# Inverse root mean squares on DVE at the end of the first product's stage, their spreading loads ahead of the second, and layer 2's weight conversion begun one stage earlier

## Chip, cores and metric

The kernel runs on one core of a Trainium2 chip. The metric is the device time of one execution in microseconds, the median of several executions.

## What is computed

Eight batches of linear attention with a root-mean-square norm, followed by two feed-forward layers over all 4608 tokens (576 of each batch):

```python
kv = np.einsum('bhsd,bhse->bhde', k, v)                  # 8 batches, 8 heads, 576 tokens, 64
out = np.einsum('bhsd,bhde->bhse', q, kv)
rms = np.sqrt(np.mean(out * out, axis=-1, keepdims=True) + 1e-06)
x = (out / rms * g_norm)                                 # then to 4608 x 512
h = x @ w_in;  x = (h * (1.0 / (1.0 + np.exp(-1.702 * h)))) @ w_out     # d_ff 2048
h = x @ w2_in; x = (h - np.tanh(h)) @ w2_out
```

## The kernel before, in words

**Blocks and stages.** The tokens are cut into eight blocks of T = 576, one for each batch; `H` is half a block, 288. The loop at the end of `body` runs over the layers `l` = 0, 1 and the blocks `n` = 0 to 7. A block has two stages: `m1` multiplies the block's operand `xo[n % 2]` with the first weights `wi`, which stay in SBUF, and applies the activation; `m2` forms the operands `jt` from the activations `GT` and multiplies them with the second weights, which come from DRAM (`wod`) through the four buffers `ST`. Both products are made with seven instead of eight sub-products, and every fp32 operand is split into two fp16 parts, so that one product is three matmuls (L702 to L704 in `m1`, L888 to L890 in `m2`). In what follows M1(n) and M2(n) are the stages of block n in the first layer; those of the second layer are named as such. The blocks n = 0 and 1 of the first layer have other stages (`m1_plain`, `m2_plain`) and are not touched.

**The side work.** Beside the stages run generators that `tick` advances: once after each step of `m1` (54 steps that tick) with the first of a generator's rates, and once after each of the 28 steps of `m2` with the second. A rate of 0.64 means 0.64 calls of `next` for each tick. In M1(n), n = 2 to 6, `front(n + 1)` makes the next batch's attention: head products (L432), numerators (L441), their squares and copies on ACT (L514, L515), and the mean squares `ms` (L448, L450, L452). Ahead of `m2` what is left of it is drained. In M2(n) `back(n + 1)` makes the norm: `roots` has ACT compute 1/sqrt and its square (L545, L546, with a table load, and a dummy activation at L626 that loads the table of the other activation again), `newton` has DVE refine it (L551, L552), POOL stores the result to the DRAM tensor `rd` (L631) and loads it back, spread over 64 partitions, in four DMAs (L638) to two buffers; after five more calls DVE multiplies each buffer into the numerators (L645), and `xprep` makes the next operand from them (DVE L343 and L356, ACT L353). At its end `fetch` begins the loads of the batch after that.

**The conversion.** `conv1` (the generator `later`) turns the second layer's 64-bit weights into fp16 pairs: 32 items, eight calls of `next` for an item, each with two loads on POOL (L147, L148, 512 KB together), ACT and DVE work (L159, L162, L163, L165, L174 to L177, L230, L180) and a store on POOL (L235, or two at L238). An item's buffer is loaded again only when the store from it has landed. It is added at the end of M1(2) with the rates 0 and 0.2; from block 3 on it has 0.64 and 0.2, from block 7 on 0.85 and 0.7. What is left of it is drained ahead of the second layer's first `m2`.

**Who sets the order.** PE and SP follow the order in which the code records them. DVE, ACT and POOL are ordered by a scheduler when the kernel is built, each engine then runs in that order, and waits where an operand or a buffer is not ready. POOL is also the queue on which the attention's inputs (`xo<-atp`, L387), the conversion's loads and stores and the `rd` transfers are issued; SP issues the weight loads `st<-wod` (L804, 512 KB each, 14 for each M2, the first four ahead of it) and the intermediate results (L870).

## Time and profile before

| | |
|---|---|
| median of 3 executions | 1542.08 us (1540.46 to 1544.48) |
| the profiled execution | 1543.9 us, of which the span of its instructions is 1542.1 us |
| PE busy in the span | 1440.5 us (93%) |
| DVE, ACT, POOL busy | 1161.3 us (75%), 896.4 us (58%), 152.7 us (10%) |
| mean granted clock of PE | 0.983 |
| chain that ended last | PE 59%, DVE 17%, DMA 12%, ACT 5%, issue 5% |
| DMA | 247.57 MB, mean 161 GB/s |

The profile is of one execution, by the hardware's profiler. Times in it are microseconds from the first instruction; a duration in a group of instructions is given in ns. Matmuls overlap, so a matmul's own duration is longer than the step from one to the next, and PE's busy share is no measure of its peak. An engine's idle time costs something only where PE comes to wait for it in the end.

### The profile page before, as it was taken

The numbers are of one execution on the slowest core, as the hardware profiler recorded it, in microseconds if no ns is written. First come the engines' busy times: TensorE is split into PE (matmuls) and PEld (weight loads), VectorE is DVE, ScalarE is ACT, GpSimd is POOL, SyncE is SP. The second block draws the span as 40 slices with busy tenths as digits, with TensorE's granted clock in tenths as the row PEclk, the third lists the DMA queues.
The fourth block names the chain that finished last, engine by engine and source line by source line (L and its number), as shares of the span: only waits on it lengthen the run. The fifth ranks groups of instructions, "written<-read, shape, count | busy, mean of one in ns | idle before, by whom it ended". The sixth has DMA issues, their size and how long they took to land.

```text
span 1542.1 us, 30058 instructions
## 1 busy us (share of the span) xinstructions
PE 1440.5 (93%) x11922; PEld 1112.3 (72%) x11922; DVE 1161.3 (75%) x2237; ACT 896.4 (58%) x1943; POOL 152.7 (10%) x238
## 2 busy tenths in 40 slices
PE   7999888979989989989889889999999999999998
PEld 5667656667766756767667667777777777777776
DVE  4998887466775866877879887777778787868585
ACT  5774554655755737657467554646555555655463
POOL 0001010010111211212122210000000000000000
PEclk9999999999999999999999999999999999999999
DMA  8767756065384572763788536151433334241504
GB/s 284 238 207 221 216 155 229 1 203 179 111 263 138 189 237 95 242 197 101 206 279 292 168 105 208 40 188 58 157 105 127 127 102 136 73 150 42 181 15 154
DMA packets 104686, 247.57 MB, mean 161 GB/s; under 512 B 10624, under 2 KB 55296, under 8 KB 104544
## 3 DMA queue, kind: packets, MB, share of 16 engines
q1 hardware_dynamic: 83504, 161.49, 32.6%
q0 software_dynamic: 21040, 84.15, 17.2%
q8 instruction: 93, 1.52, 0.4%
q14 instruction: 49, 0.40, 0.1%
HBM read 202.62 MB, written 42.98 MB: 159 GB/s over the span
## 4 chain that ended last, share of the span: by engine, by line
PE 59%; DVE 17%; DMA 12%; ACT 5%; issue 5%; POOL 1%; SPq 0%; DVEq 0%; ACTq 0%; POOLq 0%
PE X L702 6%; PE X L704 6%; PE X L703 6%; PE X L888 5%; PE X L889 5%; PE X L890 5%; DMA scratch<-rd 3%; DVE jt L783 3%; PE Z L702 3%; PE Z L703 3%; PE Z L704 3%; PE Y L888 3%; PE Y L890 3%; PE Y L889 3%; DMA wod<-cbk 2%
## 5 line engine op out<-in xcount | busy, mean ns | idle before, releaser
L783 DVE SCALAR_TENSOR_TENSOR jt<-gt,jt 128x576 f16<-128x576 f32 x420 | 312.0, 752 | 99.5 <-ACT jt L777 96.2
L777 ACT ACTIVATE jt<-gt 128x576 f16<-128x576 f32 x420 | 283.0, 682 | 163.1 <-PE X L890 57.7
L888 PE MATMUL X<-jt,st 128*128 128x288 f16 x960 | 277.5, 289 | 26.0 <-ACT mscratch L831 23.1
L889 PE MATMUL X<-jt,st 128*128 128x288 f16 x960 | 277.4, 289 | 3.7 <-DVE jt L783 3.7
L890 PE MATMUL X<-jt,st 128*128 128x288 f16 x960 | 277.2, 289 | 0.0
L702 PE MATMUL X<-xo,wi 128*128 128x288 f16 x896 | 257.7, 288 | 13.7 <-ACT mscratch L735 9.3
L703 PE MATMUL X<-xo,wi 128*128 128x288 f16 x896 | 257.6, 288 | 0.0
L704 PE MATMUL X<-xo,wi 128*128 128x288 f16 x896 | 257.6, 287 | 0.0
L889 PEld LDWEIGHTS <-st 128*128 128x128 f16 x1680 | 165.9, 99 | 70.7 <-issue 27.7
L888 PEld LDWEIGHTS <-st 128*128 128x128 f16 x1680 | 165.8, 99 | 59.0 <-DMA st<-wod 15.7
L890 PEld LDWEIGHTS <-st 128*128 128x128 f16 x1680 | 165.9, 99 | 55.6 <-issue 12.4
L703 PEld LDWEIGHTS <-wi 128*128 128x128 f16 x1568 | 153.9, 98 | 57.3 <-issue 18.5
L702 PEld LDWEIGHTS <-wi 128*128 128x128 f16 x1568 | 153.9, 98 | 53.0 <-issue 13.4
L704 PEld LDWEIGHTS <-wi 128*128 128x128 f16 x1568 | 154.0, 98 | 40.6 <-issue 1.1
L735 ACT COPY mscratch<-X 128x288 f32<-128x288 f32 x336 | 132.4, 396 | 80.4 <-PE X L704 76.3
L763 DVE TENSOR_TENSOR gt<-gt 128x576 f32<-128x576 f32 x240 | 176.5, 750 | 0.8
L740 DVE TENSOR_TENSOR mscratch<-Z,mscratch 128x288 f32<-128x288 f32 x224 | 101.7, 454 | 83.0 <-PE Z L704 42.1
L888 PE MATMUL Y<-jt,st 128*128 128x288 f16 x480 | 139.3, 290 | 10.8 <-DMA st<-wod 9.2
L889 PE MATMUL Y<-jt,st 128*128 128x288 f16 x480 | 139.2, 290 | 5.0 <-DVE jt L783 5.0
L890 PE MATMUL Y<-jt,st 128*128 128x288 f16 x480 | 139.2, 290 | 0.0
L702 PE MATMUL Z<-xo,wi 128*128 128x288 f16 x448 | 128.7, 287 | 1.7 <-ACT xo L353 1.7
L703 PE MATMUL Z<-xo,wi 128*128 128x288 f16 x448 | 128.5, 287 | 0.8 <-DVE xo L356 0.6
(249 smaller groups left out, 2495.9 us busy)
## 6 DMA issues: line engine op xcount, KB each, us to landing
st<-wod SPq DMA_DIRECT2D x210, 512.0 KB, 4.6
xo<-atp POOLq DMA_DIRECT2D x20, 640.0 KB, 5.8
scratch<-x2d SPq DMA_DIRECT2D x32, 288.0 KB, 5.5
cbk<-w_in POOLq DMA_DIRECT2D x32, 256.0 KB, 3.3
cbk<-w_out POOLq DMA_DIRECT2D x32, 256.0 KB, 3.9
scratch<-atp POOLq DMA_DIRECT2D x14, 576.0 KB, 5.4
scratch<-rd POOLq DMA_DIRECT2D x28, 288.0 KB, 8.8
x2d<-mscratch SPq DMA_DIRECT2D x28, 288.0 KB, 4.9
```

Source lines behind the costliest of these rows:

```text
L702: nc.tensor.matmul(out=out, lhsT=wh, rhs=xh, start=fresh and kt == 0, stop=False, skip_group_check=k)
L703: nc.tensor.matmul(out=out, lhsT=wh, rhs=xl, start=False, stop=False, skip_group_check=k)
L704: nc.tensor.matmul(out=out, lhsT=wl, rhs=xh, start=False, stop=kt == 1, skip_group_check=k)
L735: main(nc.scalar.copy(out=b.ap, in_=x))
L740: main(nc.vector.tensor_tensor(out=b.ap, in0=add[0], in1=b.ap, op=ALU.add))
L763: tt = lambda o, a, b: main(nc.vector.tensor_tensor(out=G[:, :, o, :], in0=G[:, :, a, :], in1=G[:, :, b, :], op=ALU.subtract))
L777: main(nc.scalar.activation(out=j[:, :, 0, :], in_=GT[STEPS2[i][1]][:, :, QD[STEPS2[i][0]], :], func=AF.Copy, scale=SX))
L783: main(nc.vector.scalar_tensor_tensor(out=j[:, :, 1, :], in0=GT[STEPS2[i][1]][:, :, QD[STEPS2[i][0]], :], scalar=SX, in1=j[:, :, 0, :], op ...
L888: nc.tensor.matmul(out=out, lhsT=wh, rhs=xh, start=a, stop=False, skip_group_check=k)
L889: nc.tensor.matmul(out=out, lhsT=wh, rhs=xl, start=False, stop=False, skip_group_check=k)
L890: nc.tensor.matmul(out=out, lhsT=wl, rhs=xh, start=False, stop=z, skip_group_check=k)
```

## The change

`inverse_roots` replaces `roots` and `newton` for the batches 3 to 7: it stands at the end of `front`, so in M1, and makes the inverse roots on DVE alone from the bits of `ms`: one integer operation (a shift and an exclusive or) and seven `scalar_tensor_tensor` of 128x288, of which the constant factor 0.375 * SG is left to the multiply in `back`. It then stores the result to `rd` and, by `broadcast`, issues the four spreading loads, which stood in `back` before. `back` keeps six calls that do nothing, the multiplies (now `scalar_tensor_tensor`) and `xprep`. Batches 1 and 2 (`back_early`) keep `roots` and `newton` and share `broadcast`. In `front` the calls without work are spread otherwise, and its rate is 0.56 instead of 0.5. `conv1` is added at the start of block 2 with the rates 0.64 and 0.2, and from block 7 on has 0.64 and 0.35. The calls of `upto` and `drain(dfr)` on the first layer's weight sums (`dfr`) change their place; that generator has ended by then, and no instruction moves for it.

```diff
--- before.py
+++ after.py
@@ -29,6 +29,7 @@
 UNITS = ((0, 0), (0, 1), (1, 0), (1, 1))
 ORDER = [2 * i + kt for kt, i in UNITS]
 CON = 226 + 8 * P + 1
+SG = 2.0 ** -66 * 1.354181
 
 
 WS = {4: 0, 1: 1, 2: 2, 5: 3, 6: 4, 3: 5, 7: 6}
@@ -502,7 +503,7 @@
                 if kt == 0:
                     kvs.append((yield from unit_kv(b, 2 + i)))
                 yield
-                yield
+            yield
             xbs[b, kt] = yield from rx.need(4 * H)
             ex = yield from rs.need(4 * H)
             og, sq = (t.ap.rearrange("p (i j n) -> p i j n", i=2, j=2) for t in (xbs[b, kt], ex))
@@ -515,10 +516,44 @@
                     nc.scalar.activation(out=og[:, i, j], in_=AT[i][:, 0:H], func=AF.Copy, scale=gsc)
                     yield
             qb.free()
+            yield
             pair_squares(kt, ex.ap)
             ex.free()
             yield
-            yield
+        yield from inverse_roots(b)
+
+    def inverse_roots(b):
+
+        y, t = (yield from rq1.need(H)), (yield from rq1.need(H))
+        stt = lambda o, a, s, b_, op0, op1: nc.vector.scalar_tensor_tensor(out=o, in0=a, scalar=s, in1=b_, op0=op0, op1=op1)
+        nc.vector.tensor_scalar(out=y.ap.bitcast(U32), in0=ms.bitcast(U32), scalar1=1, scalar2=0x7fffffff,
+                                op0=ALU.logical_shift_right, op1=ALU.bitwise_xor)
+        for k, s in enumerate((SG, 0.375 * SG)):
+            stt(t.ap, y.ap, s, ms, ALU.mult, ALU.mult)
+            stt(t.ap, y.ap, s, t.ap, ALU.mult, ALU.mult)
+            yield
+            if k == 0:
+                stt(t.ap, t.ap, -10.0 / 3.0, t.ap, ALU.add, ALU.mult)
+                stt(y.ap, t.ap, 5.0, y.ap, ALU.add, ALU.mult)
+        stt(t.ap, t.ap, -3.0, y.ap, ALU.add, ALU.mult)
+        y.free()
+        nc.gpsimd.dma_start(out=rd[b], in_=t.ap)
+        t.free()
+        yield
+        yield from broadcast(b, rq1)
+
+    def broadcast(b, other):
+
+        rows = rd[b].rearrange("(g r) n -> r g n", r=32)
+        rbs[b] = []
+        for kt, reg in ((0, rs), (1, other)):
+            t = yield from reg.need(4 * H)
+            for c in range(2):
+                nc.gpsimd.dma_start(out=t.ap[c * HD:(c + 1) * HD, :].rearrange("p (g n) -> p g n", g=4),
+                                    in_=rows[2 * kt + c].partition_broadcast(HD))
+            rbs[b].append(t)
+
+    rbs = {}
 
     def unit0(u):
 
@@ -594,20 +629,13 @@
         nc.gpsimd.dma_start(out=rd[b], in_=t.ap)
         t.free()
         yield
-        rows = rd[b].rearrange("(g r) n -> r g n", r=32)
-        rb = []
-        for kt, reg in ((0, rs), (1, rq0)):
-            t = yield from reg.need(4 * H)
-            for c in range(2):
-                nc.gpsimd.dma_start(out=t.ap[c * HD:(c + 1) * HD, :].rearrange("p (g n) -> p g n", g=4),
-                                    in_=rows[2 * kt + c].partition_broadcast(HD))
-            rb.append(t)
+        yield from broadcast(b, rq0)
         for _ in range(5):
             yield
         for kt in range(2):
-            o = xbs[b, kt].ap
-            nc.vector.tensor_tensor(out=o, in0=rb[kt].ap, in1=o, op=ALU.mult)
-            rb[kt].free()
+            o, rb = xbs[b, kt].ap, rbs[b][kt]
+            nc.vector.tensor_tensor(out=o, in0=rb.ap, in1=o, op=ALU.mult)
+            rb.free()
             yield
             if b == 1:
                 yield from xprep0(xbs[b, kt], dst[:, kt])
@@ -618,32 +646,12 @@
 
     def back(b, dst):
 
-        yield
-        yield
-        yield
-        yt[:] = (yield from rq1.need(H)), (yield from rq1.need(H))
-        roots(slice(0, P))
-        nc.scalar.activation(out=dummy, in_=yt[1].ap[:, 0:1], func=AF.Gelu_apprx_sigmoid)
-        yield
-        newton(slice(0, P))
-        y, t = yt
-        y.free()
-        nc.gpsimd.dma_start(out=rd[b], in_=t.ap)
-        t.free()
...
-        for _ in range(5):
+        for _ in range(6):
             yield
         for kt in range(2):
-            o = xbs[b, kt].ap
-            nc.vector.tensor_tensor(out=o, in0=rb[kt].ap, in1=o, op=ALU.mult)
-            rb[kt].free()
+            o, rb = xbs[b, kt].ap, rbs[b][kt]
+            nc.vector.scalar_tensor_tensor(out=o, in0=rb.ap, scalar=0.375 * SG, in1=o, op0=ALU.mult, op1=ALU.mult)
+            rb.free()
             yield
             ex = yield from rs.need(3 * H)
             yield from xprep(xbs[b, kt], ex, dst[:, kt])
@@ -1108,19 +1116,18 @@
                 elif n == 1:
                     bk = add_side(both(2, xo[0]), 0.75, 0.85)
                 elif n < NS - 1:
-                    fr = add_side(front(n + 1), 0.5, 0.0)
+                    fr = add_side(front(n + 1), 0.56, 0.0)
                 else:
                     bk = add_side(x2load(0, xo[0]), 0.4, 0.8)
             elif n < NS - 1:
                 bk = add_side(x2load(n + 1, xo[(n + 1) % 2]), 0.4, 0.8)
-            if (l, n) == (0, 3):
-                rate(later, 0.64, 0.2)
+            if (l, n) == (0, 2):
+                drain(dfr)
+                add_side(later, 0.64, 0.2)
             if (l, n) == (0, 7):
-                rate(later, 0.85, 0.7)
+                rate(later, 0.64, 0.35)
 
             def hook(p):
-                if (l, n) == (0, 2):
-                    upto(p + 2)
                 if p >= 2 and p % 2 == 0:
                     jcap[0] = (1, 2, 5)[p // 2 - 1]
                     jadvance(jcap[0])
@@ -1177,12 +1184,7 @@
                     marks.clear()
                     marks.update({k: m for k, m in latest.items() if k == ENG.DVE})
                 man.enter_context(tc.manual_schedule(engines=frozenset([ENG.PE, ENG.SP])))
-                if (l, n) == (0, 2):
-                    upto(2)
                 tails = m1(l, n, hook)
-            if (l, n) == (0, 2):
-                drain(dfr)
-                add_side(later, 0.0, 0.2)
             jcap[0] = 5
             if (l, n) == (1, 0):
                 drain([later])
```

The change moves instructions through the scheduler. The rows below are the order in which an engine runs them, of the program before and of the changed one. The changed program has its own line numbers: L748 is L740 of before, L771 is L763, L791 is L783, L388 is L387, L453 is L452, L148 and L149 are L147 and L148, L236 is L235, and L163, L164, L166, L175 to L178 and L181 are the conversion's L162, L163, L165, L174 to L177 and L180.

DVE at the end of M1(2), before (L740 adds of `m1`, L763 and L783 the first operands of `m2`, L452 the mean squares of batch 3):

```order
L763 TENSOR_TENSOR gt_75<-gt_75 128x2x288
L452 TENSOR_TENSOR ms<-AT,ms 128x288
L763 TENSOR_TENSOR gt_75<-gt_75 128x2x288
L740 TENSOR_TENSOR mscratch<-Z_86,mscratch 128x288 x2
L740 TENSOR_TENSOR mscratch<-Y_85,mscratch 128x288
L740 TENSOR_TENSOR mscratch<-Z_87,mscratch 128x288
L783 SCALAR_TENSOR_TENSOR jt<-gt_76,jt 128x2x288 x2
```

The same place in the changed program (L528 and L529 are the inverse roots, `cbk` the conversion):

```order
L453 TENSOR_TENSOR ms<-AT,ms 128x288
L791 SCALAR_TENSOR_TENSOR jt<-gt_75,jt 128x2x288
L529 TENSOR_SCALAR scratch<-ms 128x288
L181 TENSOR_TENSOR cbk<-cbk 128x7x128
L528 SCALAR_TENSOR_TENSOR scratch<-scratch,ms 128x288
L791 SCALAR_TENSOR_TENSOR jt<-gt_75,jt 128x2x288
L748 TENSOR_TENSOR mscratch<-Z_87,mscratch 128x288
L528 SCALAR_TENSOR_TENSOR scratch<-scratch 128x288
L748 TENSOR_TENSOR mscratch<-Y_84,mscratch 128x288
L528 SCALAR_TENSOR_TENSOR scratch<-scratch 128x288
L771 TENSOR_TENSOR gt_75<-gt_75 128x2x288
L528 SCALAR_TENSOR_TENSOR scratch<-scratch 128x288
```

Seven of `m1`'s adds follow the mean squares now, five before. The eight operations of the inverse roots (three of them behind the last row shown) and pieces of the conversion stand between these adds, and two adds follow the last of the eight.

DVE in M2(2), where the first multiply of the norm stands, before (the multiply is L645):

```order
L825 SCALAR_TENSOR_TENSOR mscratch<-Y_85,mscratch 128x288
L783 SCALAR_TENSOR_TENSOR jt<-gt_75,jt 128x2x288
L763 TENSOR_TENSOR gt_76<-gt_76 128x2x288
L783 SCALAR_TENSOR_TENSOR jt<-gt_76,jt 128x2x288
L783 SCALAR_TENSOR_TENSOR jt<-gt_73,jt 128x2x288
L783 SCALAR_TENSOR_TENSOR jt<-gt_74,jt 128x2x288
L645 TENSOR_TENSOR scratch<-scratch 128x1152
```

and in the changed program (the multiply is L653):

```order
L791 SCALAR_TENSOR_TENSOR jt<-gt_74,jt 128x2x288
L771 TENSOR_TENSOR gt_76<-gt_76 128x2x288
L771 TENSOR_TENSOR gt_73<-gt_73 128x2x288
L791 SCALAR_TENSOR_TENSOR jt<-gt_75,jt 128x2x288
L771 TENSOR_TENSOR gt_74<-gt_74 128x2x288
L791 SCALAR_TENSOR_TENSOR jt<-gt_76,jt 128x2x288
L653 SCALAR_TENSOR_TENSOR scratch<-scratch 128x1152
```

Before, the multiply stood behind the operand of step 17 of the 28 and behind the stage's first results (L825); now it stands behind the operand of step 11 and ahead of those results.

POOL from the end of M1(2) into M2(2), before (`xo<-atp` are the next batch's keys and values, which may be loaded to `xo` only when M1's last matmuls have read it):

```order
L387 DMA xo_71<-atp 128x1280 x3
L631 DMA rd<-scratch 128x288
L638 DMA scratch<-rd 64x4x288 x4
L387 DMA scratch<-atp 128x1152 x2
L387 DMA xo_71<-atp 128x1280
```

and in the changed program:

```order
L540 DMA rd<-scratch 128x288
L388 DMA xo_71<-atp 128x1280
L552 DMA scratch<-rd 64x4x288 x4
L388 DMA xo_71<-atp 128x1280 x2
L236 DMA wid<-cbk 128x1792
```

The store to `rd` stands ahead of the three key loads, the four spreading loads behind the first of them and ahead of the other two. In block 4 the two loads of a conversion item, in block 5 those and the second key load stand between as well; in block 6 there are no key loads.


## Rows read from the trace of the kernel before

**Rows 1.** Windows: length, busy (count) of PE, PEld, DVE, ACT, POOL, clock, DMA share, GB/s

```profile
311.60:365.30 53.70, 45.23 (x350) 35.07 (x348) 38.49 (x65) 27.02 (x48) 5.71 (x10) 0.90 0.73 225
416.10:468.20 52.10, 44.72 (x350) 34.84 (x348) 41.73 (x76) 27.97 (x51) 7.71 (x13) 0.93 0.82 257
518.80:568.90 50.10, 44.65 (x350) 34.47 (x348) 36.88 (x64) 25.71 (x46) 7.70 (x13) 0.97 0.79 247
623.50:671.00 47.50, 44.53 (x350) 34.62 (x349) 39.28 (x70) 26.96 (x49) 7.73 (x13) 0.96 0.81 267
721.80:771.80 50.00, 44.26 (x351) 34.64 (x349) 40.52 (x72) 27.98 (x50) 7.51 (x11) 0.97 0.65 191
568.90:623.50 54.60, 49.93 (x454) 35.47 (x452) 36.23 (x75) 37.68 (x96) 8.42 (x13) 0.97 0.35 116
771.80:818.60 46.80, 41.77 (x326) 32.42 (x324) 35.97 (x79) 31.67 (x78) 14.11 (x21) 0.96 0.81 283
818.60:862.90 44.30, 42.78 (x350) 33.96 (x348) 41.52 (x78) 24.59 (x45) 10.98 (x15) 1.00 0.82 265
862.90:908.60 45.70, 41.60 (x327) 32.50 (x326) 40.99 (x95) 31.39 (x75) 9.03 (x13) 0.96 0.36 108
908.60:960.10 51.50, 44.74 (x350) 34.77 (x349) 36.90 (x66) 23.56 (x43) 3.65 (x5) 0.93 0.56 188
1042.40:1082.20 39.80, 39.80 (x327) 31.73 (x326) 30.76 (x67) 24.37 (x62) 0.72 (x1) 1.00 0.15 49
1082.20:1124.80 42.60, 42.60 (x350) 34.03 (x348) 33.72 (x59) 22.61 (x41) 2.13 (x3) 1.00 0.54 178
```

**Rows 2.** Waits from 260 or 311 to 960: us in total, times, longest

```profile
PE X L888 <- ACT mscratch L831: 21.6, 3, 8.5
DVE scratch L645 <- DMA scratch<-rd: 34.4, 8, 9.6
ACT cbk L159 <- DMA cbk<-w_out: 12.5, 2, 7.9
```

**Rows 3.** The chain that ended last, M2(2): start, us, what

```profile
325.84 4.87 DMA rd<-scratch
331.91 8.06 DMA scratch<-rd
344.79 0.40 ACT mscratch L831
```

**Rows 4.** Timeline of PE: matmuls that waited, in order of time

```profile
571.10 0.28 PE L702 MATMUL Z<-xo,wi 128*128 128x288 f16 x1 [1.65 <-ACT xo L353]
657.71 0.42 PE L888 MATMUL Y<-jt,st 128*128 128x288 f16 x1 [2.75 <-DMA st<-wod]
800.43 0.28 PE L702 MATMUL X<-xo,wi 128*128 128x288 f16 x1 [4.91 <-ACT mscratch L735]
867.93 0.28 PE L702 MATMUL X<-xo,wi 128*128 128x288 f16 x1 [4.10 <-ACT mscratch L831]
920.05 0.42 PE L888 MATMUL Y<-jt,st 128*128 128x288 f16 x1 [6.50 <-DMA st<-wod]
```

**Rows 5.** L631, the five stores to rd

```profile
DMA to landing us min/median/max: 2.5/4.6/8.0
```

**Rows 6.** L804, the weight load issued at 634.0 in M2(5)

```profile
DMA to landing us min/median/max: 6.0/6.0/6.0
```

**Rows 7.** Timeline of PE: start, us, what, wait before; the matmul that needed that load

```profile
640.09 0.30 PE L888 MATMUL Z<-jt,st 128*128 128x288 f16 x1 [0.22 <-DMA st<-wod]
```

**Rows 8.** L804, three weight loads beside the spreading loads in M2(5)

```profile
L804 SPq DMA_DIRECT2D st<-wod x3: 319/319/319, 643.2 to 649.1; - x3
DMA to landing us min/median/max: 8.4/9.8/11.5
```

**Rows 9.** Groups by line, 260 to 960: out<-in, shapes, count, busy us, mean ns, idle before

```profile
L725 DVE SCALAR_TENSOR_TENSOR gt<-mscratch,gt 128x288 f32<-128x288 f32 x24 | 10.2, 450 | 0.0
```

**Rows 10.** Windows, columns as in rows 1: the end of M1(3)

```profile
405.00:416.00 11.00, 10.62 (x91) 7.93 (x89) 8.68 (x19) 7.89 (x21) 1.97 (x3) 1.00 0.24 84
```

8 lines of the change are left out of this document (removed).

## Prediction

> **What bounds the kernel now.** First the table of stages [rows 1]: a stage of the second layer without a wait is the yardstick, 39.8 us for M1 and 42.6 us for M2, PE busy throughout and at full clock. The first layer's M2(2) to M2(6) take 53.7, 52.1, 50.1, 47.5 and 50.0 us, 253.4 us together where five clean ones take 213.0. M1(5) takes 54.6, M1(7) 46.8 and M2(7) 44.3; the second layer's M1(0) takes 45.7 and its M2(0) 51.5. That is where time can be won; the other stages of the second layer have nothing to give.
>
> Next the waits [rows 2]: DVE stands 34.4 us, in eight waits, ahead of the norm's multiply (L645) until a spreading load lands, and PE stands 21.6 us in three waits for ACT to empty a bank of X (L831). The chain [rows 3] ties the two: in M2(2) the store to `rd` lands after 4.87 us, the loads take 8.06 us more, and only behind the multiply and `xprep` comes the ACT copy that lets PE go on. PE does not wait for the roots themselves; it waits for two DMAs in a row that are begun too late in M2, through two engines that run in order. Last, single waits [rows 4]: 1.65 us at the start of M1(5), 2.75 us in M2(5), 4.91 us in M1(7), 4.10 us at the start of the second layer's M1(0), 6.50 us in its M2(0). The last three belong to the conversion: ACT twice waits for a load of it, 12.5 us together [rows 2], and the second layer's first weights cannot be loaded before the conversion's last store.
>
> The sum is made against the profiled execution, 1543.9 us, and carried to the median, 1542.1 us, which lies 1.8 us lower.
>
> **1. M2(2) to M2(6).** The store and the spreading loads now begin at M1's end. A store lands 2.5 to 8.0 us after its issue, 4.6 at the median [rows 5], and a second load of the pair some 8.1 us after its own [rows 3]. The multiply stands at step 11 of the 28, and its DVE row is reached some 12 us into M2 (28 steps in 42.6 us are 1.5 us each, and DVE runs ahead of PE by up to five steps). Store at M2's start, plus 4.6, plus the POOL issue, plus 8.1: about 13 us. So DVE waits for 0 to 2 us there, and PE's 21.6 us of waits and M2(4)'s, which come from it, go. I take them as gone.
>
> What is late next is the weight loads. The spreading loads are moved on POOL past two of the three key loads, so in the first 10 us of M2(2) to M2(5) all of them, the spreading loads and the first weights share the DMA engines. A weight load at that place landed 6.0 us after its issue in M2(5), and PE had waited for it for 0.22 us [rows 6, 7]: PE leaves it 5.8 us. Weight loads issued beside the spreading loads took 8.4 to 11.5 us, 9.8 at the median [rows 8]; there PE had slack and still stood 2.75 us [rows 4]. Bounds for the new wait: 0 if the weights are not held up, 8.4 - 5.8 = 2.6, 9.8 - 5.8 = 4.0, at most 11.5 - 5.8 = 5.7 us. I take 3.3, between the shortest and the median, since fewer weight loads are in flight at once. A wait of that size costs clock as well: M2(5) is 47.5 us, PE is idle for 47.5 - 44.5 = 3.0 of it, and 47.5 - 3.0 - 42.6 = 1.9 us are the granted clock of 0.96 [rows 1]. So M2(2) to M2(5) become 42.6 + 3.3 + 1.9 = 47.8 us each. M2(6) has no key loads; 43.6, with 1 us for smaller waits. Together 4 x 47.8 + 43.6 = 234.8: **-18.6 us**.
>
> A rule speaks against that wait. The Trainium skill, page "DMA: Bandwidth & Descriptors", section "Queues, rings and completion order", says that a DMA engine takes turns between the queues it has work for, packet by packet; then a weight load on SP's queue would not stand behind POOL's. The landings of [rows 8] speak against equal turns, since a weight load would then take about twice its own time and not 5 us more. The first rival below is what the rule would give.
>
> **2. Start of M1(5).** The late `xprep` of M2(4) holds PE for 1.65 us [rows 4], and the clock of 0.97 over 54.6 us costs 1.6 [rows 1]. With the multiply early both go: **-3.3 us** (0 to -3.3).
>
> **3. The roots in M1.** Eight DVE operations of at most 0.45 us [rows 9] are 3.6 us for each of five stages. Over M1 they are covered (DVE was busy 8.7 of 11 us even at its end [rows 10]), but there only 2.3 us are free: 1.3 us run over, onto `m1`'s last adds and the first operands. PE may feel 0 to 1.3 us of it; 0.5 in five stages, **+2.5 us**. ACT loses five pairs of root and square and their table loads, DVE two operations in M2; neither is on the chain once the loads are early, so I cost that at nothing. Conversion in M1(2) is work on DVE and ACT that M1(3) already carries with no wait of over 1.2 us; nothing.
>
> **4. Conversion.** Calls until the second layer, 260 being needed: before 5.6 + 4 x 40.2 + 65.5 = 231.7, now 5 x 40.2 + 44.4 = 245.4. An item in M1(7) now takes 8 / 0.64 = 12.5 steps instead of 9.4; 3.1 steps of about 0.75 us are 2.3 us more for a load that came 4.91 us late through a DMA that is busy at 0.81 [rows 1, 4]: **-2.3 us** (0 to -6.8, the clock with it). M2(7), with half as many calls: **-1.0 us** (0 to -1.7). The second layer's M1(0): the ACT wait of 7.9 us [rows 2] for the load at its start goes, since the item before it has twice the time; 45.7 becomes 40.5, **-5.2 us** (0 to -5.9). Its M2(0): the last store lies behind some 23 of 54 steps of M1(0) instead of at its end, so the four first weight loads are done well before; 51.5 becomes 42.6, **-8.9 us** (0 to -8.9).
>
> Sum: -18.6 - 3.3 + 2.5 - 2.3 - 1.0 - 5.2 - 8.9 = -36.8. 1543.9 - 36.8 = 1507.1 for an execution like the profiled one, 1505.3 against the median: **1505.3 us**, with 1497 to 1514 for this case alone.
>
> **Rivals.**
>
> *The weights are not held up.* The two queues share, or the spreading loads are through before the fifth weight load. Terms 1 lose 4 x (3.3 + 1.9) = 20.8 us more: 1484.5. For it: M2(7) runs at a DMA share of 0.82 and loses 1.5 us of PE time in all [rows 1]. Against it: [rows 8]. Chance 0.22.
>
> *The spreading loads still land late.* In POOL's order they stand behind a key load that waits for M1's last matmul, in blocks 4 and 5 behind conversion loads too, and the store before them can take 8.0 us [rows 5]. If the multiply waits as it did, terms 1 and 2 are nothing: 1505.3 + 18.6 + 3.3 = 1527.2. Against it: the store is issued over 12 us earlier than in the chain of [rows 3]. Chance 0.17.
>
> *The change does not bring what it says.* As the last, and the second layer's M2(0) still waits for the conversion's end, because its items slip against the count of calls: 1527.2 + 8.9 = 1536, or with more slip no difference. Chance 0.07.
>
> *Slower: M2 becomes bound by DMA.* 257 GB/s over the 52.1 us of M2(3) are 13.4 MB [rows 1]. Nothing of it is taken away, and M2 is to be shorter. With 18.2 us won outside term 1, the kernel is slower once M2(2) to M2(5) take over (253.4 + 18.2 - 43.6) / 4 = 57.0 us each: once the DMA gives under 235 GB/s there. M2(2) had 225; at that rate they take 59.6 us, and the time is 1542.1 - 18.2 + (4 x 59.6 + 43.6 - 253.4) = 1552.5. Against it: 267 GB/s in M2(5) and 283 in M1(7) [rows 1]. Chance 0.05.
>
> **Numbers.** The forecast has 0.49. The range, 1481 to 1528, holds it and the first two rivals: it ends 3.5 us below the first and 0.8 us above the second, and some 0.15 of all the chance lies beyond (a part of each of the two, and the last two rivals). About 0.3% is what a measurement of this kernel tells from no change, so faster means under 1537.5 and slower over 1546.7. Faster: the forecast, the first two rivals and a little of the third, 0.90; same 0.05; slower 0.05.
>
> **What would show it.** DVE's wait at the multiply falls from 34.4 to under 10 us. PE's wait for L831 in M2(2) to M2(6) is gone, and waits for `st<-wod` of 2.6 to 5.7 us stand at the fifth weight load, some 15 us into M2(2) to M2(5), with a fall of the clock behind each; M2(6) has none. M1(5) is some 51 us. The second layer's M1(0) and M2(0) are 40 to 41 and 43 us. Weight waits missing, or stages of 44 us, would be the first rival; a DVE wait of over 4 us in each stage the second. The prediction is wrong if M2(2) to M2(6) add up to over 245 us or under 220.

## The result, and the profile after

The changed kernel takes 1503.55 us (1500.06 to 1504.44, four executions) where the kernel before takes 1541.27 us (1538.06 to 1544.48, a fourth execution added to the three of the table): a ratio of 0.9751, with a 95% interval of 0.9725 to 0.9778, or 37.7 us less. The forecast was 1505.3 us, 36.8 us less.

The profiled execution is the fastest of the four, 1500.06 us, with a span of 1498.3 us; it lies 43.8 us below the profiled one of before, so the stages below add up to more than the medians' 37.7. Windows of the changed kernel, columns as in [rows 1], in this order: M2(2) to M2(6), M1(5), M1(7), M2(7), the second layer's M1(0) and M2(0), then M1(2), M1(3), M1(4) and M1(6).

```profile
312.40:360.20 47.80, 44.36 (x350) 34.43 (x348) 40.89 (x75) 25.60 (x47) 7.75 (x13) 0.96 0.85 273
408.30:455.50 47.20, 44.58 (x351) 34.67 (x349) 41.98 (x75) 25.95 (x48) 8.45 (x14) 0.96 0.83 280
503.90:553.60 49.70, 44.80 (x350) 34.66 (x348) 40.12 (x71) 24.95 (x45) 9.69 (x16) 0.97 0.83 262
603.50:654.00 50.50, 44.93 (x351) 34.72 (x349) 43.54 (x79) 25.67 (x46) 11.69 (x18) 0.97 0.87 276
702.40:745.10 42.70, 42.70 (x351) 34.01 (x349) 41.65 (x76) 24.73 (x45) 7.42 (x11) 1.00 0.70 225
553.60:603.50 49.90, 47.92 (x454) 34.65 (x452) 33.89 (x72) 34.96 (x91) 8.45 (x12) 1.00 0.36 114
745.10:790.30 45.20, 40.34 (x326) 31.63 (x324) 33.78 (x73) 31.63 (x76) 12.79 (x19) 1.00 0.83 278
790.30:833.80 43.50, 42.83 (x351) 33.99 (x349) 40.11 (x73) 25.32 (x48) 8.01 (x11) 1.00 0.81 268
833.80:873.70 39.90, 39.86 (x327) 31.70 (x325) 33.83 (x75) 26.15 (x66) 1.52 (x2) 1.00 0.25 82
873.70:916.30 42.60, 42.60 (x350) 34.03 (x348) 33.73 (x59) 22.61 (x41) 2.14 (x3) 1.00 0.55 175
262.10:312.40 50.30, 48.87 (x461) 35.31 (x460) 31.63 (x68) 34.31 (x90) 6.49 (x10) 1.00 0.32 104
360.20:408.30 48.10, 47.72 (x455) 34.67 (x453) 33.71 (x70) 34.13 (x89) 8.49 (x13) 1.00 0.36 118
455.50:503.90 48.40, 47.87 (x454) 34.64 (x452) 33.23 (x73) 34.79 (x91) 7.92 (x12) 1.00 0.35 113
654.00:702.40 48.40, 47.79 (x454) 34.63 (x452) 31.83 (x68) 35.10 (x91) 10.97 (x15) 1.00 0.37 107
```

The last four stages of the kernel before, which the prediction did not show:

```profile
260.30:311.60 51.30, 48.84 (x461) 35.36 (x459) 18.81 (x35) 30.41 (x80) 0.55 (x1) 1.00 0.14 45
365.30:416.10 50.80, 48.28 (x455) 34.68 (x453) 31.68 (x66) 34.68 (x91) 8.44 (x13) 1.00 0.32 102
468.20:518.80 50.60, 48.27 (x455) 34.67 (x454) 32.18 (x67) 35.34 (x91) 8.43 (x13) 1.00 0.34 114
671.00:721.80 50.80, 48.61 (x455) 34.67 (x453) 34.68 (x70) 36.08 (x94) 11.43 (x16) 1.00 0.39 118
```

M2(2) to M2(6) fall from 253.4 to 237.9 us. M1(2) to M1(6) fall from 258.1 to 245.1 us. M1(7), M2(7) and the second layer's first two stages, "the four stages" below, fall from 188.3 to 171.2 us. The first 260 us, which the change leaves as they were, are 1.8 us longer in this execution; why is open (in the profiled executions of the kernels below they differ by up to 5 us). -15.5 - 13.0 - 17.1 + 1.8 = -43.8.

Waits of the changed kernel from 311 to 960 us, columns as in [rows 2]; L896 is a matmul of `m2`, L653 the norm's multiply, L160 the conversion's first step on ACT:

```profile
PE Z L896 <- DMA st<-wod: 16.3, 7, 5.0
DVE scratch L653 <- DMA scratch<-rd: 10.4, 3, 5.3
ACT cbk L160 <- DMA cbk<-w_out: 8.8, 3, 4.4
```

PE's 21.6 us of waits for ACT to empty X [rows 2] are gone. What stands in their place is what the prediction named, weight loads. The longest of them in M2(2), M2(3), M2(4) and M2(5), in PE's timeline with the columns of [rows 4]:

```profile
332.38 0.42 PE L896 MATMUL Z<-jt,st 128*128 128x288 f16 x1 [2.71 <-DMA st<-wod]
427.33 0.41 PE L896 MATMUL Z<-jt,st 128*128 128x288 f16 x1 [2.62 <-DMA st<-wod]
525.47 0.30 PE L896 MATMUL Z<-jt,st 128*128 128x288 f16 x1 [2.93 <-DMA st<-wod]
625.40 0.42 PE L896 MATMUL Z<-jt,st 128*128 128x288 f16 x1 [5.05 <-DMA st<-wod]
```

They end some 20 us into the stage, not 15: they stand not at the fifth weight load, which has 0.73 us in M2(2) and 1.61 us in M2(4), but at the sixth. M2(6), which has no key loads, has none and takes 42.7 us. The mean granted clock of the four stages with such a wait is 0.96 or 0.97, that of M2(6) 1.00.

Why the weights are late can be seen in the DMA queues, here from 322 to 328 us in M2(2), while weight loads were outstanding on SP's queue (q1), and the spreading loads, two key loads and a conversion store on POOL's (q0); the columns are packets, MB, and the time of their packets as a share of 16 engines:

```profile
q0 software_dynamic: 347, 1.37, 95.3%
q1 hardware_dynamic: 36, 0.12, 7.0%
```

POOL's queue has the engines almost alone here, and in M2(5), where a weight load is outstanding from 614.5 to 625.4 us, it has 99.5% from 615 to 618 us. But that does not last: from 622 to 626 us in M2(5) the two queues have about the same.

```profile
q1 hardware_dynamic: 191, 0.70, 52.9%
q0 software_dynamic: 141, 0.62, 49.3%
```

The Trainium skill, page "DMA: Bandwidth & Descriptors", section "Queues, rings and completion order", has an engine take turns between the queues it has work for, packet by packet. The second of these stretches agrees with it, with 53% and 49%; the first shows no such turns, with 95% against 7%. Whether SP's packets were ready and passed over there, or were not there yet, no row tells.

### The profile page after: what moved, and what is told of

Its sections match the earlier page's. It is cut to its first block, busy times and chain, and to the rows that moved or that the text cites. A ratio compares the mean times of both kernels' runs of the same rounds, so it can differ in the third digit from the quotient of the medians.

```text
span 1498.3 us, 30084 instructions
## 1 busy us (share of the span) xinstructions
PE 1431.6 (96%) x11922; PEld 1108.8 (74%) x11922; DVE 1170.0 (78%) x2267; ACT 881.6 (59%) x1918; POOL 153.2 (10%) x238
## 3 DMA queue, kind: packets, MB, share of 16 engines
q0 software_dynamic: 21040, 84.15, 17.7%
## 4 chain that ended last, share of the span: by engine, by line
PE 71%; DVE 12%; DMA 8%; issue 5%; ACT 4%; SPq 0%; POOL 0%; DVEq 0%; POOLq 0%; ACTq 0%
PE X L896 7%; PE X L898 7%; PE X L897 7%; PE X L710 6%; PE X L712 6%; PE X L711 6%; PE Y L896 4%; PE Y L898 4%; PE Y L897 3%; DMA st<-wod 3%; PE Z L710 3%; PE Z L712 3%; PE Z L711 3%; DVE jt L791 2%; PE Z L896 2%
## 5 line engine op out<-in xcount | busy, mean ns | idle before, releaser
L791 DVE SCALAR_TENSOR_TENSOR jt<-gt,jt 128x576 f16<-128x576 f32 x420 | 312.6, 754 | 74.7 <-ACT jt L785 71.3
L896 PE MATMUL X<-jt,st 128*128 128x288 f16 x960 | 274.5, 286 | 4.5 <-ACT gt L938 1.7
L897 PE MATMUL X<-jt,st 128*128 128x288 f16 x960 | 274.5, 286 | 2.9 <-DVE jt L791 2.9
L898 PE MATMUL X<-jt,st 128*128 128x288 f16 x960 | 274.5, 286 | 0.0
L896 PEld LDWEIGHTS <-st 128*128 128x128 f16 x1680 | 165.3, 98 | 64.3 <-DMA st<-wod 21.9
L898 PEld LDWEIGHTS <-st 128*128 128x128 f16 x1680 | 165.3, 98 | 49.4 <-issue 7.0
L710 PEld LDWEIGHTS <-wi 128*128 128x128 f16 x1568 | 153.3, 98 | 52.2 <-issue 13.4
L771 DVE TENSOR_TENSOR gt<-gt 128x576 f32<-128x576 f32 x240 | 176.7, 751 | 1.6 <-ACT gt L717 1.2
L748 DVE TENSOR_TENSOR mscratch<-Z,mscratch 128x288 f32<-128x288 f32 x224 | 101.7, 454 | 75.1 <-PE Z L712 40.7
L896 PE MATMUL Y<-jt,st 128*128 128x288 f16 x480 | 137.3, 286 | 2.0 <-ACT gt L938 1.3
L897 PE MATMUL Y<-jt,st 128*128 128x288 f16 x480 | 137.3, 286 | 0.4 <-DVE jt L791 0.4
L898 PE MATMUL Y<-jt,st 128*128 128x288 f16 x480 | 137.3, 286 | 0.0
```

The lines of the kernel that those rows point to most:

```text
L710: nc.tensor.matmul(out=out, lhsT=wh, rhs=xh, start=fresh and kt == 0, stop=False, skip_group_check=k)
L748: main(nc.vector.tensor_tensor(out=b.ap, in0=add[0], in1=b.ap, op=ALU.add))
L771: tt = lambda o, a, b: main(nc.vector.tensor_tensor(out=G[:, :, o, :], in0=G[:, :, a, :], in1=G[:, :, b, :], op=ALU.subtract))
L791: main(nc.vector.scalar_tensor_tensor(out=j[:, :, 1, :], in0=GT[STEPS2[i][1]][:, :, QD[STEPS2[i][0]], :], scalar=SX, in1=j[:, :, 0, :], op ...
L896: nc.tensor.matmul(out=out, lhsT=wh, rhs=xh, start=a, stop=False, skip_group_check=k)
L897: nc.tensor.matmul(out=out, lhsT=wh, rhs=xl, start=False, stop=False, skip_group_check=k)
```

## The experiments

All runs are told against the kernel before on the same chip. M1 and M2 are the sums of M1(2) to M1(6) and of M2(2) to M2(6) in the profiled execution, "four" the sum of the four stages, "store" the issue of the store to `rd` after the start of M2(2) to M2(6), in us, taken from the trace.

| kernel | median us | ratio, 95% interval | M1 | M2 | four | store, M2(2) to M2(6) |
|---|---|---|---|---|---|---|
| before | | | 258.1 | 253.4 | 188.3 | 14.2, 14.2, 16.9, 14.9, 15.4 |
| changed | 1503.55 | 0.9751, 0.9725 to 0.9778 | 245.1 | 237.9 | 171.2 | 1.4, 1.4, 1.3, 2.3, 1.9 |
| e1, old conversion | 1508.74 | 0.9784, 0.9763 to 0.9805 | 242.6 | 233.4 | 186.8 | -2.7, 1.5, -0.7, 1.9, 3.3 |
| e2, conversion alone | 1530.57 | 0.9913, 0.9889 to 0.9938 | 254.7 | 254.2 | 177.0 | 14.3, 15.1, 14.3, 15.0, 15.9 |
| e3, roots on ACT | 1491.89 | 0.9678, 0.9655 to 0.9701 | 258.5 | 218.8 | 171.0 | -3.4, -1.7, -4.7, -4.3, -7.0 |
| e4, old front | 1507.72 | 0.9784, 0.9764 to 0.9805 | 255.0 | 238.3 | 168.8 | 3.0, 3.9, 4.3, 5.0, 4.6 |
| e5, front 0.62 | 1483.11 | 0.9630, 0.9607 to 0.9652 | 247.1 | 221.9 | 169.2 | -3.7, -1.7, -1.6, -2.5, -1.8 |
| e6, front 0.70 | 1480.90 | 0.9615, 0.9591 to 0.9640 | 247.1 | 218.6 | 170.4 | -4.3, -5.2, -4.5, -7.7, -4.9 |
| e7, keys late | 1481.00 | 0.9609, 0.9587 to 0.9631 | 247.4 | 220.5 | 169.2 | 1.3, 1.5, 1.3, 2.3, 1.9 |
| e8, both | 1476.52 | 0.9579, 0.9558 to 0.9600 | 248.2 | 215.1 | 168.6 | -4.3, -5.3, -4.5, -7.6, -5.0 |
| e9, both, even conversion | 1474.54 | 0.9557, 0.9536 to 0.9578 | 249.9 | 215.8 | 165.3 | -5.3, -4.0, -5.9, -3.9, -4.9 |
| e10, 0.70, old conversion | 1498.55 | 0.9719, 0.9697 to 0.9741 | 244.9 | 220.2 | 190.1 | -9.1, -4.9, -4.0, -5.3, -4.4 |
| e11, 0.70, old spreading | 1491.20 | 0.9705, 0.9658 to 0.9752 | 255.5 | 221.0 | 172.4 | -7.5, -5.7, -6.5, -6.6, -4.9 |
| e12, 0.50, new spreading | 1500.96 | 0.9768, 0.9727 to 0.9808 | 250.7 | 233.1 | 169.7 | 3.0, 5.1, 5.1, 5.8, 4.5 |

### The parts apart: e1 and e2

e1 is the changed kernel with the conversion's place and rates of before:

```diff
             if (l, n) == (0, 2):
                 drain(dfr)
-                add_side(later, 0.64, 0.2)
+            if (l, n) == (0, 3):
+                rate(later, 0.64, 0.2)
             if (l, n) == (0, 7):
-                rate(later, 0.64, 0.35)
+                rate(later, 0.85, 0.7)
...
                 tails = m1(l, n, hook)
+            if (l, n) == (0, 2):
+                add_side(later, 0.0, 0.2)
```

> The changed kernel with the conversion of before (added at the end of M1(2), rates 0.64/0.2 from block 3, 0.85/0.7 from block 7); roots in M1 and early spreading loads stay. My theory, that the two parts add up and do not touch each other: M1(7), M2(7), the second layer's M1(0) and M2(0) go back to what they were before (46.8, 44.3, 45.7, 51.5 us; in the changed kernel 45.2, 43.5, 39.9, 42.6), so 17 us more than the changed kernel, about 1520.6 us, with M2(2) to M2(6) still near 238 us together. Rival, that the conversion's loads and stores at the start of M2 are what holds the weight loads up: M2(2), which then has no conversion traffic, loses its waits for st<-wod, and the time is below 1516 us.

e2 is the kernel before with the change's lines for the conversion (and its place of the calls on `dfr`), and nothing else of the change.

> The kernel before with the changed conversion alone (begun in M1(2) with 0.64/0.2, from block 7 0.64/0.35); roots on ACT in M2 and late spreading loads as before. My theory of independent parts: the 17 us of the four stages around the change of layer and no more, 1541.3 - 17 = about 1524 us; the DVE wait at the multiply stays at 30 to 40 us. Rival, that the early conversion only pays where M2 is shorter (more of its items then slip past the change of layer): the second layer's M2(0) keeps a wait of over 3 us for st<-wod, and the time is over 1532 us.

In e1 the four stages cost what they should, 15.6 us more than in the changed kernel, but the median is only 5.2 us higher: M2 is 4.5 us and M1 2.5 us shorter (by the profiled executions, of which the changed kernel's is its fastest, e1 is 6.4 us longer). The rival's number came true, below 1516 us, but not by its reason alone: M2(2) is 4.9 us shorter, M2(4) and M2(5) 2.5 and 2.7 us, while M2(3) and M2(6) are 2.9 and 2.4 us longer. In M2(2) the store is issued 2.7 us ahead of the stage instead of 1.4 us behind it, and M2(2) takes 42.9 us, not 47.8. What moved the store is seen on DVE. The changed kernel at the end of M1(2), with the conversion (`cbk`) between the roots (L529, the first; L528):

```profile
304.16 0.30 DVE L529 TENSOR_SCALAR scratch<-ms 128x288 uint32<-128x288 uint32 x1
304.38 1.08 DVE L181 TENSOR_TENSOR cbk<-cbk 128x896 f16<-128x896 f32 x1
...
313.04 0.44 DVE L528 SCALAR_TENSOR_TENSOR scratch<-scratch 128x288 f32<-128x288 f32 x1
313.40 0.28 DVE L175 TENSOR_TENSOR cbk<-cbk 128x128 f32<-128x128 f32 x1
```

and e1, without it:

```profile
300.23 0.30 DVE L529 TENSOR_SCALAR scratch<-ms 128x288 uint32<-128x288 uint32 x1
...
305.59 0.45 DVE L528 SCALAR_TENSOR_TENSOR scratch<-scratch 128x288 f32<-128x288 f32 x1
305.95 0.75 DVE L771 TENSOR_TENSOR gt<-gt 128x576 f32<-128x576 f32 x1
307.78 0.46 DVE L748 TENSOR_TENSOR mscratch<-Z,mscratch 128x288 f32<-128x288 f32 x1 [1.07 <-PE Z L712]
```

From the first to the last root it is 9.3 us with the conversion and 5.8 us without, 3.5 of the 4.1 us between the stores; only in e1 does DVE then wait for PE again.

e2 gains 11 us, not 17: of the four stages the second layer's M1(0) and M2(0) fall to 39.9 and 42.6 us as in the changed kernel, but M1(7) rises to 50.6 us. PE waits there 2.5 us for the operand that M2(6) prepared, whose spreading loads land 32.1 to 37.3 us into M2(6) (25.2 to 32.4 us in the kernel before), and 3.3 us behind ACT, which waits 4.9 us for a load of the conversion. So the two parts are not independent: the conversion alone is worth less while the transfers are late, and early transfers are worth less while the conversion crowds DVE.

### Is it DVE, ACT, or the time of the store: e3

```diff
-        yield from inverse_roots(b)
+        yt[:] = (yield from rq1.need(H)), (yield from rq1.need(H))
+        roots(slice(0, P))
+        nc.scalar.activation(out=dummy, in_=yt[1].ap[:, 0:1], func=AF.Gelu_apprx_sigmoid)
+        yield
+        newton(slice(0, P))
...
+        yield from broadcast(b, rq1)
```

The multiply in `back` is a `tensor_tensor` again, as before the change.

> The changed kernel with the inverse roots made as before (ACT reciprocal root and square with two table loads, two operations on DVE) but at the place of the change, the end of M1, with the store and the spreading loads where the change has them. My theory, that only the place of the two transfers matters and the engine does not: within 3 us of the changed kernel, 1501 to 1506 us. Rival, that the two table loads of 1.28 us and the two operations of 0.44 us, 3.6 us of ACT at a place where it has to empty the banks of M1, hold PE up: 2 to 4 us more in each of M1(2) to M1(6), 1512 to 1524 us, with waits of PE for ACT at the end of M1 or the start of M2.

Both theories missed: e3 takes 1491.89 us, some 12 us less than the changed kernel. The rival's price is there, M1 is 13.4 us longer in five stages, and PE waits for ACT's copy out of X, in the waits of e3 from 255 to 745 us:

```profile
PE X L720 <- ACT mscratch L753: 12.9, 10, 2.8
```

But M2 is 19.1 us shorter. The roots on ACT are ready earlier, the store goes out 1.7 to 7.0 us ahead of M2, the last spreading load lands 6.2 to 10.0 us into M2 (14.8 to 22.5 us in the changed kernel), and the weights are not held up. Here the engine that makes the roots matters less than when their store goes out.

### The time of the store: e5 and e6

One number each is changed in the changed kernel:

```diff
-                    fr = add_side(front(n + 1), 0.56, 0.0)
+                    fr = add_side(front(n + 1), 0.62, 0.0)
```

> The changed kernel with one number changed, the rate of front: 0.62 instead of 0.56, so that the roots stand one to two of M1's adds earlier on DVE. In the changed kernel the store to rd is issued 1.3 to 1.9 us behind the start of M2; with the roots on ACT it was issued 1.7 to 6.9 us ahead of it, the spreading loads were nearly through when the key loads and the weights came, and M2(2) to M2(6) took 219 us together instead of 238. Theory one, that only the time of the store decides: the store comes 0 to 3 us ahead of M2, M2(2) to M2(5) fall from 48.8 to some 45 us on average, and the time is 1485 to 1494 us. Theory two, that DVE makes the difference, whose roots between M1's adds delay the rest: the M2 stages stay within 1.5 us of the changed kernel's, 1499 to 1506 us. Theory three, that a faster front makes PE wait in M1 for the attention's copies: M1 stages over 50 us, the time 1500 us or more although M2 is short.

> As the run with 0.62, with the rate of front 0.70: the roots stand three or more of M1's adds earlier. Theory one, that only the time of the store decides: M2(2) to M2(6) are 43 to 44 us each (218 us together), and with M1 as in the changed kernel the time is 1483 to 1487 us. Theory two, DVE itself: 1499 to 1506 us. Theory three, that the faster front costs in M1: M1(2) to M1(6) 1 to 3 us longer each than in the changed kernel, the time 1488 to 1500 us, and slower than with 0.62.

Theory one holds, with both medians, 1483.11 and 1480.90 us, some 2 us below its ranges. The store is issued 1.6 to 3.7 us ahead of M2 with 0.62 and 4.3 to 7.7 us with 0.70. M2(2) to M2(5) with 0.70:

```profile
311.30:355.30 44.00, 42.94 (x350) 33.86 (x348) 39.99 (x74) 25.60 (x46) 6.64 (x12) 1.00 0.88 301
404.10:447.40 43.30, 42.82 (x350) 33.97 (x349) 40.49 (x72) 25.33 (x47) 6.43 (x11) 1.00 0.88 302
496.40:541.00 44.60, 42.79 (x351) 33.95 (x349) 40.09 (x69) 25.06 (x46) 7.23 (x13) 1.00 0.84 294
590.10:634.10 44.00, 42.73 (x349) 33.92 (x348) 41.52 (x75) 25.39 (x47) 8.10 (x13) 1.00 0.88 293
```

The faster front costs 2 us in M1, on balance all of it in M1(2) and M1(3), and with 0.70 it pays 19 us in M2, with 0.62 16 us. Stages that run at 293 to 302 GB/s and full clock also show that the changed kernel's 262 to 280 GB/s were not all that the DMA can give there.

### What the weights collide with: e7

```diff
-        nc.gpsimd.dma_start(out=t.ap[:, 0:n], in_=atp[b - 1, kt, :, a:a + n])
+        (e or nc.gpsimd).dma_start(out=t.ap[:, 0:n], in_=atp[b - 1, kt, :, a:a + n])
...
+            if b < NS - 1:
+                keys.setdefault(b + 1, []).append((yield from unit_kv(b + 1, kt)))
```

with `nc.sync` as `e` for the first three key loads of the batches 4 to 7.

> The changed kernel with the three key loads of batches 4 to 7, 640 KB each, taken from POOL's queue at the start of M2 and put on SP's, the first behind the ninth weight load of M2 and the others behind the twelfth; the spreading loads stay where the change has them. Theory one, that the spreading loads and the key loads together, one behind the other on POOL's queue, hold the weight loads up: M2(2) to M2(5) fall to the 43 to 44 us of M2(6), which has no key loads, 20 us less in all, 1482 to 1488 us with up to 1 us more in each M1 whose first keys come later. Theory two, that the spreading loads alone do it: waits for st<-wod of over 2 us stay in M2(2) to M2(5), 1498 to 1506 us. Theory three, that the key loads cost the same wherever they stand in M2: the waits move to the tenth to thirteenth weight load, M2 at 46 to 48 us, 1494 to 1500 us.

Theory one: 1481.00 us, though the store goes out as late as in the changed kernel, 1.3 to 2.3 us into M2. M2(2), M2(3) and M2(5):

```profile
309.90:352.70 42.80, 42.80 (x351) 33.95 (x349) 40.83 (x75) 25.60 (x47) 6.09 (x10) 1.00 0.85 297
400.70:444.60 43.90, 43.24 (x351) 33.99 (x350) 41.37 (x76) 25.94 (x48) 6.69 (x11) 1.00 0.84 287
589.30:634.60 45.30, 43.15 (x351) 33.97 (x349) 43.22 (x79) 25.74 (x46) 10.04 (x15) 1.00 0.88 287
```

The spreading loads alone do not hold the weights up by more than 1.8 us; with the key loads behind them on the same queue they do. The edit changes the key loads' time and their queue at once; which of the two counts was not tried.

### Both, and the rest: e8, e9, e10

e8 has the edits of e6 and e7 together.

> The changed kernel with the rate of front at 0.70 and the three key loads on SP's queue in the middle of M2 as well. Each alone took about 22 us off the changed kernel (1480.9 and 1481.0 us). Theory one, that both remove the same collision at the start of M2: little is left to win, M2(2) to M2(6) at 42.6 to 43.5 us each, 3 to 6 us less than either alone, 1475 to 1479 us. Theory two, that they remove different waits: together well below 1472 us. Theory three, that the earlier conversion, left as it is, limits what remains (M1(7), M2(4) and M2(5)): no difference to either alone, 1480 to 1482 us.

1476.52 us: theory one. Each edit alone removes the same collision, and both together leave 42.7 to 43.8 us for each M2, some 4 us less in the median than either alone, with intervals that overlap a little.

e9 spreads the conversion otherwise in e8:

```diff
-                add_side(later, 0.64, 0.2)
+                add_side(later, 0.70, 0.2)
             if (l, n) == (0, 7):
-                rate(later, 0.64, 0.35)
+                rate(later, 0.45, 0.35)
```

> As the run before it, with the conversion spread otherwise: rate 0.70 instead of 0.64 in M1(2) to M1(6), 0.45 instead of 0.64 in M1(7). M1(7) still has 3.5 us of PE idle time, waits of ACT for the conversion's loads. Theory one, that those waits come from the pace of the items in M1(7): they go, M1(7) 40.5 to 41.5 us instead of 43.9, the other stages as they were, 2 to 3 us less than the run before it. Theory two, that M1(7)'s DMA is full whatever the conversion does there: no change in M1(7); and the faster items in M1(2) to M1(6) cost 0.5 to 1 us each there, so up to 5 us more.

M1(7) does as theory one has it, and more, from 43.4 us in e8 to a stage in which PE does not wait, at a DMA share of 0.88:

```profile
727.80:767.70 39.90, 39.90 (x327) 31.73 (x326) 32.01 (x67) 30.10 (x74) 11.32 (x17) 1.00 0.88 302
```

M1 before it is 1.7 us longer, as theory two had it. 1474.54 us is the fastest median here, but its interval overlaps that of e8.

e10 is e1 with the rate 0.70.

> The changed kernel with the rate of front at 0.70 and the conversion of before. With the rate of the change (0.56) the conversion of before cost only 5 us more than the changed one, not the 17 us of the four stages, because M2(2), M2(4), M2(5) were shorter with it. Theory one, that without the conversion in M1(2) the roots come earlier on DVE there, and that the rate of 0.70 does the same by itself: now the full price of the four stages shows, 1480.9 + 13 to 17 = 1494 to 1498 us. Theory two, that less conversion traffic in M2 itself is what counts: again some 5 us, 1485 to 1488 us.

1498.55 us, 17.7 us above e6, a little past theory one's range: with the store early in every block the old conversion costs its full price, 19.7 us in the four stages (M1(7) 48.4, M2(0) of the second layer 51.4), and M2 differs by 1.6 us. With the store early in both, the old conversion does not shorten M2: theory one. So e10 speaks for the time of the store, and against the conversion's traffic in M2, as the cause of e1's 4.5 us; e1's M2(5), 2.7 us shorter with its store only 0.4 us earlier, does not fit in. M2 is not all of the difference between 5.2 and 17.7 us: M1(7) is 2.6 us shorter in e1 than in e10, and by the profiled executions some 5 us lie in the first 260 us, which the edit does not touch.

### What shortened M1: e4, e11, e12

e4 puts the calls without work in `front` back where they were, and the rate to 0.50:

```diff
                 yield
-            yield
+                yield
...
             qb.free()
-            yield
             pair_squares(kt, ex.ap)
             ex.free()
             yield
+            yield
```

> The changed kernel with the calls of front spread as before and its rate 0.5 instead of 0.56. In the profile M1(3), M1(4) and M1(6) are 2.1 to 2.7 us shorter than before, where I had forecast 0.5 us more. Theory one, that the new pace does it (the copies of the numerators no longer keep PE waiting, L515 before): with the old pace these stages, M1(2) and M1(5) have their waits back, 8 to 11 us more than the changed kernel, 1511 to 1515 us. Theory two, that it comes from elsewhere (a shorter M2 leaves DVE and ACT less in arrears at the start of M1, or the conversion is at another place): within 2 us of the changed kernel, or slower only because the spreading loads start later, which would show in the DVE wait at the multiply and not in M1.

e11 has the old calls with 0.70, e12 the new ones with 0.50.

> The run with the rate of front at 0.70, but the calls without work in front as before the change (two behind each head product, none ahead of the mean squares, two behind them). With the old calls and 0.50 the stages M1(3), M1(4), M1(6) took 50.7, 51.5, 51.8 us, with the changed calls and 0.56, 0.62 or 0.70 about 48.0 to 49.0. Theory one, that the place of the calls decides (without the call ahead of the mean squares PE comes to them before ACT has squared the numerators): M1(3), M1(4), M1(6) at 50.5 to 52 us again, 6 to 9 us more than the run with 0.70, 1487 to 1490 us, with waits of PE for ACT's L515 or L516. Theory two, that the rate decides: 48.5 to 49.5 us each, 1479 to 1483 us.

> The changed kernel with the rate of front at 0.50 as before, but the changed spreading of the calls kept. Theory one, that the place of the calls decides M1: M1(3), M1(4), M1(6) stay at 48 to 49 us; the store to rd is issued later than in the changed kernel, so M2(2) to M2(6) have weight waits or DVE waits, and the time is 1500 to 1512 us. Theory two, that the rate decides M1: these stages take 50.5 to 52 us, and the time is 1507 to 1515 us.

In e4 M1 is 9.9 us longer than in the changed kernel, in e11 8.4 us longer than in e6: theory one of each, by the stages. (e4's median is only 4.2 us higher: its four stages are 2.4 us shorter, and the changed kernel's profiled execution lies 3.5 us below its median, e4's 1.4 us. By the median alone theory one would have failed. e11's median is 10.3 us above that of e6, 1 us past theory one's range.) The waits of PE for ACT's copies of the numerators (L515 and L516), from 260 to 772 us. The kernel before (L448 the mean squares, L441 the numerators):

```profile
PE AT L448 <- ACT scratch L515: 5.4, 6, 1.6
PE AT L441 <- ACT scratch L515: 1.2, 2, 0.7
```

the changed kernel (L442 the numerators):

```profile
PE AT L442 <- ACT scratch L516: 0.7, 2, 0.4
```

e4 (L449 the mean squares), which has them back:

```profile
PE AT L449 <- ACT scratch L516: 6.0, 6, 1.5
PE AT L442 <- ACT scratch L516: 1.9, 3, 0.7
```

e11, which has the old calls with the faster rate:

```profile
PE AT L442 <- ACT scratch L516: 7.7, 10, 1.7
PE AT L449 <- ACT scratch L516: 4.6, 9, 1.1
```

and e12, where the waits at the mean squares are gone and those at the numerators are larger:

```profile
PE AT L442 <- ACT scratch L516: 5.6, 5, 1.5
```

The call ahead of the mean squares removes PE's wait there: the runs that have it show none, or a single one of 0.4 us (e9, e10). In e12 M1 lies between, 250.7 us, so the rate has a part in it too: the calls alone are worth 4.3 us at the rate 0.50 (e4 against e12) and 8.4 us at 0.70 (e11 against e6). e12's median is not told apart from the changed kernel's: M1 is 5.6 us longer, M2 4.8 us shorter, although its store is issued later, 3.0 to 5.8 us into M2. Where the key loads stay on POOL's queue, M2(2) to M2(5) take 42.6 to 47.2 us with the store ahead of M2 (e1, e3, e5, e6, e10, e11) and 44.7 to 50.5 us with the store behind its start (the changed kernel, e1, e4, e12). Within either group the earlier store is not always the better: e11's M2(5), with the store 6.6 us ahead, has 46.7 us, e5's M2(2), with 3.7 us, has 43.1, and e4, with the store as late as e12, has 238.3 us in all. Why is left open.

## Why the prediction was right, and where it was not

**1. M2(2) to M2(6): right in its mechanism and near in size.** Forecast 234.8, measured 237.9 us. The wait for ACT is gone; new waits for `st<-wod` stand in M2(2) to M2(5) and none in M2(6); the 47.8 us taken for each of the four are 47.8, 47.2, 49.7 and 50.5. The size taken from [rows 8], 3.3 us of wait, is 2.6 to 5.05 us for the longest ones, and the 1.9 us of clock from [rows 1] are 1.8 to 2.3 us, worked out in the same way. The place was off: the wait is not at the fifth load but at the sixth. M2(6) won 0.9 us more than forecast. The step that the multiply waits 0 to 2 us was too low for two stages, M2(2) with 3.1 and M2(4) with 5.3 us of the 10.4, as the second load of the first pair landed 12.1 to 18.6 us into M2 and not at 13. That is because the store is issued 1.3 to 2.3 us into M2, not at its start, and because the spreading loads themselves take 10.4 us at the median there, in place of the 8.1 of [rows 3]. No wait of PE in these stages is put down to it.

The reason given against turns between the queues does not follow from its rows. The weight loads of the kernel before took, by the last number, 4.6 us at the median from issue to landing:

```profile
st<-wod SPq DMA_DIRECT2D x210, 512.0 KB, 4.6
```

The 8.4 to 11.5 us of [rows 8] are about twice that, which is what turns would give, and not a sign against them. The wait that was forecast came about, but it was not well argued against its rival.

**The first rival is what the experiments made of the kernel.** "The weights are not held up", 1484.5 us, is e5, e6 and e7: 1483.11, 1480.90 and 1481.00 us. Its condition, that the spreading loads are through before the weights are needed, was not met at the rate 0.56 and is met at 0.62. e7 gets there without it: its last spreading loads land 14.0 to 17.8 us into M2(2) to M2(5), and what is gone from there is the key loads. By the stages it is less exact: it has 234.8 - 20.8 = 214.0 us for M2(2) to M2(6), and these three have 218.6 to 221.9, e8 215.1; M1's unforeseen gain makes up for it. What the prediction did not see is how near the two cases lay to each other: 3 to 5 us in the time of the store (e5).

**2. Start of M1(5): right.** The wait of 1.65 us at its first matmuls and the loss of clock are gone; 54.6 became 49.9 us, 4.7 instead of 3.3 less. Where the further 1.4 us come from is open: they are not owed to the calls of `front`, since e4, with the old ones, has 49.6 us.

**3. The rest of M1: wrong in sign, the largest miss.** The step "PE may feel 0 to 1.3 us of it; 0.5 in five stages, +2.5 us" was measured as -1.0, -2.7, -2.2 and -2.4 us in M1(2), M1(3), M1(4) and M1(6). The price of the roots themselves was not far off: e4, which has them in M1 with the calls and the rate of before, takes 153.9 us in M1(3), M1(4) and M1(6) where the kernel before takes 152.2, so 0.6 us more in each. And they do run over, as the working said, onto the store as well. What the prediction left out of its sum without a reason is the respread calls of `front` and its rate: together 9.9 us over the five stages (e4). "Conversion in M1(2) ... nothing" was wrong as well: without it M1(2) is 1.1 us shorter (e1 against the changed kernel) and 2.1 us shorter (e10 against e6), and in e1 the store is earlier and M2(2) 4.9 us shorter.

**4. Conversion: right.** Forecast -2.3, -1.0, -5.2, -8.9 us; measured -1.6, -0.8, -5.8, -8.9. e10 confirms the price of the four stages in the median, 17.7 us. That ACT still waits 8.8 us for the conversion's loads, and that M1(7) is 45.2 us, means that its items were still too fast there; in e9, with 0.45 there and 0.70 in the blocks before, 1.5 us of ACT's waits are left and PE has none in M1(7).

**The sum: in part luck.** By the stages of the profiled executions M1(2) to M1(6) won 13.0 us where the terms have 0.8, M2(2) to M2(6) 15.5 where they have 18.6, the four stages 17.1 where they have 17.4. That makes 45.6 us, 43.8 with the first 260 us, and not 36.8; for an execution like the profiled one the forecast, 1507.1 us, was 7 us too long. That the median is within 2 us of the forecast rests on the other three executions of the changed kernel, which take 2.7 to 4.4 us longer than the profiled one, and to the profiled one of before, which lies 2.6 us above the median there. In which stages those three are longer is not known.

**The slower rival did not come about.** M2(2) to M2(5) had 262 to 280 GB/s, above the 235 from which it would have decided, and up to 304 GB/s in e8's M2(2) with full clock.

## What to carry to other kernels

When a transfer is moved ahead of a stage boundary, ask not only whether it starts earlier but what else becomes ready at that boundary: here a store some 3 to 10 us earlier still, or key loads over 20 us later, was worth some 20 us on top of the 38 of the change. Find what sets the moment of issue (here a vector engine crowded by side work) and price that, not only what the compute engine feels. And price every edit of a generator's calls without work: where they stand decides which engine waits.
